# An FFT filter and two MLPs in one kernel: constants on another queue, the first weight pair and the filter's imaginary part loaded later

## The chip, the cores and the metric

One core of a Trainium2 chip runs the whole program in one launch. The metric is the device time of that launch in microseconds (us), as the median of several runs. Engines are named TensorE (PE in profiles), VectorE (DVE), ScalarE (ACT), GpSimd (POOL) and SyncE (SP, which here issues DMAs).

## The reference, cut to what matters

```python
# x: (2, 3008, 256); filt_r, filt_i: (1505, 256); w_in: (256, 2048); w_out: (2048, 256)
X = np.fft.rfft(x, axis=1)
y = np.fft.irfft(X * (filt_r + 1j * filt_i)[None], n=3008, axis=1)
x = y.reshape(6016, 256)
h = x @ w_in                       # first MLP
x = np.maximum(0.01 * h, h) @ w_out
h = x @ w_in2                      # second MLP, its own weights
out = np.maximum(h, 0.0) ** 2 @ w_out2
```

The MLP weights arrive as double precision numbers; the kernel receives them as pairs of 32-bit words.

## The kernel before, in words

The kernel has a filter phase and an MLP phase, and the MLP phase starts as soon as the filter's last results are there.

**Filter phase.** The transform of length 3008 is done as 47 x 64. The work is cut into 32 units: 16 groups of 16 channels (`q`), two batches each, in the order of `units`. A loop over passes `s` (L639) runs the units as a pipeline, so that pass `s` holds different stages of several units:

- `load_x(s + 3)`: SP issues the input of a unit three passes ahead, as two DMAs (L509), into one of four buffers.
- `stage_a(s)` (L538): TensorE's input transform, which needs the input; `stage_r(s)` (L545): VectorE transposes the result (tile `bin`).
- `stage_b(s - 1)` (L550): TensorE, into `px`, with the constant `cb`; `stage_s(s - 1)`: ScalarE copies `px` (L558 in two halves or L560), and VectorE multiplies it with the filter's real part `fr` (L562).
- `stage_2(s - 2)` (L568): GpSimd multiplies the copy with the imaginary part `fi`; `stage_y(s - 2)` (L575) adds the products for some units.
- `stage_i(s - 3)` (L580, L582): TensorE's inverse transform, with the constants `ci` and `cs`; `stage_t(s - 4)` (L589): VectorE transposes the result into `zin`.
- from the middle on also `stage_o` (L596, with the constant `dd`) and `stage_w`: the last transform and its copy, which yields the MLP's input.

The imaginary part needs a sign for each frequency and group before it is used. For groups 0 to 3 that is one product with the constant `sg` in `sign_f` (L530, on VectorE for groups 1 and 2, otherwise on GpSimd); for the larger pieces it is 24 ScalarE steps per piece in `sign_k` (L534). `FI` says which groups form a piece and in which pass it is loaded (L521); `SIGN` says in which pass its sign steps begin and how many a pass has.

**Weights.** Each of the eight weight pairs of an MLP is converted from double precision to single precision and split into a high and a low part. `load_w` (L179, SP) loads one half of a pair, 512 KB, into one buffer per half. `narrow_w` gives the steps: `size` (L200, ScalarE: absolute value), `upper` (L204, L205, VectorE), `signed` (L208, VectorE), `exp` (L213, VectorE), `low` (L219, VectorE; it then has SP load the same half of the next pair), `add` (L225) and `sums` (L230 to L233), then `hi` (L258, ScalarE) and `lo` (L262). The first five pairs are converted during the filter phase.

**What sets the order.** Every engine works through its own instructions in the order in which the program writes them. A clock with four ticks a pass (`tick("F")`) puts the steps of the conversions between the stages: a step goes at the start tick of its pair (`STARTS`) plus its offset in the table `NARROW_F`, and each tick issues the steps that are due:

```python
STARTS = (0, 24, 53, 76, 101)
NARROW_F = dict(
    size0=8, upper0=10, signed0=13, exp0=17, low0=18, size1=18, add0=21, upper1=22, sums=26, signed1=26,
    hi_i=32, exp1=32, low1=33, lo_i=34, add1=40, hi_o=45, lo_o=46,
)
```

Ahead of the loop SP issues the first table `ra` (L490), the inputs of units 0 to 4, the constants (L621, L622, L626, L627, L634), the first pieces of `fr` and `fi`, and both halves of the first weight pair.

**MLP phase.** TensorE multiplies blocks of up to 512 tokens with the weights in three products each (`up`, L342, and `down`, L444), and ScalarE, VectorE and GpSimd prepare and finish the operands around them.

Of the kernel before, what the change touches and what calls it, by code (L numbers as in the profile page):

```python
# [43 lines left out]
SWAP_V = (3, 16, 17, 18, 20, 21, 25, 26, 27, 29, 30)  # L44


FI = ((2, 4, 2), (4, 8, 2), (8, 16, 7))
SGN = (1, 2)
SIGN = ((4, 8, 4, 4), (8, 16, 9, 3))


H0 = 3
# [6 lines left out]


TM = 8
STARTS = (0, 24, 53, 76, 101)
STARTS_1 = (0, 16, 32)
NARROW_F = dict(
    size0=8, upper0=10, signed0=13, exp0=17, low0=18, size1=18, add0=21, upper1=22, sums=26, signed1=26,
# [77 lines left out]
def fft_filter_then_two_mlps(  # L143
# [15 lines left out]
    nc = tc.nc  # L159
# [17 lines left out]
    def load_w(layer, p, k):  # L177
        raw = ws_p.tile([P, 512, 2], I32, tag=f"wraw{k}", name=f"wraw{k}")
        nc.sync.dma_start(  # L179
            raw.rearrange("p c t -> p (c t)"),  # L180
            w_src[layer][p, :, k * 512 : (k + 1) * 512].bitcast(I32),
        )
        w_raw[layer, p, k] = raw
# [90 lines left out]
    def begin(c, steps, table, start):  # L274

        due[c].extend((start + t, steps[name]) for name, t in table.items())
# [21 lines left out]
    def load_macro(l, m, load=True):  # L298
        t0, n = macros[m]
        x = x_p.tile([P, 2, 2, TT], F32, tag="x", name="x")  # L300
        if load:
            nc.sync.dma_start(
                x[:, :, :, :n],
                x_src[l][:, :, t0 : t0 + 2 * n].rearrange("p k (t n) -> p k t n", t=2),
            )
        s = x_p.tile([P, 3, TT], F32, tag="xs", name="xs")
        b11, b12, b21, b22 = (x[:, k, t, :n] for k in range(2) for t in range(2))
        t1, t2, t4 = (s[:, k, :n] for k in range(3))
        x_ops[l, m] = {}
        x_f32[l, m] = {"b11": b11, "b12": b12, "b21": b21, "b22": b22, "t1": t1, "t2": t2, "t3": b12, "t4": t4}  # L310
        return x

    def sum_macro(l, m, part, eng):
        t, a, b = (("t1", "b12", "b11"), ("t2", "b22", "t1"), ("t3", "b22", "b12"), ("t4", "b21", "t2"))[part]
        x = x_f32[l, m]
        eng.tensor_tensor(x[t], x[a], x[b], ALU.subtract)
# [147 lines left out]
    with ExitStack() as fctx:  # L464
# [13 lines left out]
        cb = fc.tile([P, P], F32, name="cb")  # L478
        ci = fc.tile([P, P], F32, name="ci")
        cs = fc.tile([P, P], F32, name="cs")  # L480
        sg = fc.tile([P, NK], F32, name="sg")
        dd = fc.tile([P, P], F32, name="dd")
# [22 lines left out]
        def load_x(s):  # L505
            b, q = units[s]
            t = xin_p.tile([2 * N1, UC * NJ], F32, tag="xin", name="xin")
            for r0, r1 in ((0, XR), (XR, 2 * N1)):
                nc.sync.dma_start(t[r0:r1], x[b, r0:r1, q * UC * NJ : (q + 1) * UC * NJ])  # L509
            xin[s] = t  # L510

        def load_fr(q):
            fr_sb[q] = f_p.tile([P, UC, NK], F32, tag="fr", name="fr")
            nc.sync.dma_start(fr_sb[q], fr[:, q * UC : (q + 1) * UC, :])
# [17 lines left out]
        def sign_k(q0, q1, k):  # L532
            t = fi_of(q0, q1)[:, :, k]
            nc.scalar.activation(t, t, AF.Copy, scale=sg[:, k : k + 1])  # L534

        def stage_a(s):
            pa = ps_a.tile([P, UC, NJ], F32, tag="pa", name="pa")
            nc.tensor.matmul(  # L538
                pa.rearrange("p c n -> p (c n)"), ra[: 2 * N1], xin.pop(s), start=True, stop=True
            )  # L540
            pas[s] = pa
# [6 lines left out]
        def stage_b(s):  # L548
            px = ps_x.tile([P, UC, NK], F32, tag="px", name="px")
            nc.tensor.matmul(px, cb, bin_.pop(s)[:, :, :NK], start=True, stop=True)  # L550
            xps[s] = px
# [49 lines left out]
        def stage_w(h, j, eng):  # L601
            pi = pis.pop((h, j))[:, :, : 2 * N1]
            copy = (lambda d, s: nc.scalar.activation(d, s, AF.Copy)) if eng is nc.scalar else eng.tensor_copy  # L603
            t0, nt = j * TO, TO
            if t0 + nt <= 2 * TT:
                copy(x0[:, h, t0 : t0 + nt].rearrange("p (i t) -> p i t", i=4), pi)
                return
            o = xw_p.tile([P, TO], F32, tag="xo", name="xo")
            copy(o.rearrange("p (i t) -> p i t", i=4), pi)
            a = max(0, 2 * TT - t0)  # L610
            if a:
                nc.gpsimd.tensor_copy(x0[:, h, t0 : t0 + a], o[:, :a])
            nc.sync.dma_start(xt[:, h, t0 + a : t0 + nt], o[:, a:])
# [2 lines left out]
        TO = 8 * N1  # L616
        NO = NT // TO
        x0 = load_macro(0, 0, load=False).rearrange("p k t n -> p k (t n)")
        load_x(0)
        load_x(1)  # L620
        nc.sync.dma_start(cb, c_cb)  # L621
        nc.sync.dma_start(sg, c_sg)  # L622
        load_fr(0)
        load_fi(0, 1)
        load_x(2)
        nc.sync.dma_start(ci, c_ci)  # L626
        nc.sync.dma_start(cs, c_cs)  # L627
        load_x(3)
        load_w(0, 0, 0)
        load_fr(1)  # L630
        load_fi(1, 2)
        load_x(4)
        load_w(0, 0, 1)
        nc.sync.dma_start(dd, c_dd)  # L634
        n = len(units)
        h0 = w0 = 0
        for k, t in enumerate(STARTS):
            begin("F", narrow_w(0, k, f"F{k}"), NARROW_F, t)
        for s in range(n + 4):  # L639
            if 2 <= s < n - 3:  # L640
                load_x(s + 3)
            if s < n:
                stage_a(s)
            if 1 <= s <= n:
                stage_b(s - 1)
            if s > n // 2 + H0 and w0 < h0:
                stage_w(0, w0, nc.scalar)
                w0 += 1
                if w0 == 5:
                    sum_macro(0, 0, 0, nc.gpsimd)  # L650
            tick("F")
            if 4 <= s:
                stage_t(s - 4)
            if 2 <= s <= n + 1:
                stage_2(s - 2)
            tick("F")
            if s < n:
                stage_r(s)
            if 2 <= s <= n + 1:
                stage_y(s - 2)  # L660
            tick("F")
            if 1 <= s <= n:
                stage_s(s - 1)
            if 3 <= s <= n + 2:
                stage_i(s - 3)
            if s % 2 == 0 and s // 2 + 2 < NU:
                load_fr(s // 2 + 2)
            for i, (a, b, t) in enumerate(FI):
                if s == t:
                    load_fi(a, b)  # L670
            if s % 2 == 0 and s // 2 < FI[1][0]:
                sign_f(s // 2)
            for q0, q1, t, c in SIGN:
                for k in range(max(0, (s - t) * c), min(NK, (s - t + 1) * c)):
                    sign_k(q0, q1, k)
            if s >= n // 2 + H0:
                for k in range(1 if s < n else DRAIN[s - n]):
                    if h0 < NO:
                        stage_o(0, h0, ps_a, "pa")
                        h0 += 1  # L680
            tick("F")
# [120 lines left out]
```

## Time and profile before

| | us |
|---|---|
| median of 3 runs | 1157.0 |
| lowest and highest run | 1156.37 and 1157.23 |
| the profiled execution | 1158.98 |
| its span, first to last instruction | 1157.2 |
| TensorE busy | 1135.9 (98%) |
| GpSimd, VectorE, ScalarE busy | 764.9, 654.0, 649.7 |

The rows of a profile come from one execution. A busy time is the sum of an engine's instructions in a stretch. An idle time that stands with an instruction is what its engine waited ahead of it, with the instruction or DMA that ended the wait. The chain of waits goes back from the last instruction, at each step to what released it or to the one ahead of it on its engine. A granted clock of 1.00 is TensorE's full 2.4 GHz, 0.50 is 1.2 GHz.

### The profile page before, as it was taken

The page shows a single profiled execution, that of the slowest core. Times are in us where ns is not written, and L with a number is a line of the kernel's source. Part 1 is how long each engine was busy: PE and PEld are TensorE (multiplying, and loading weights), DVE is VectorE, ACT ScalarE, POOL GpSimd, SP SyncE. Part 2 cuts the span into 40 slices and gives each one's busy share as a digit, 9 for nine tenths or more (in the row PEclk, how much of TensorE's full clock was granted, in tenths as well). Part 3 has the DMA queues.
Part 4 walks back from the last instruction along what each step waited for, and adds up shares of the span by engine and source line. Part 5 has one row for each costly group of instructions (what it writes and reads, how often), then busy time and mean ns, then how long its engine had stood idle before and what let it go on. Part 6 is the DMA issues. An engine that isn't in the chain of part 4 may idle for free.

```text
span 1157.2 us, 14009 instructions
## 1 busy us (share of the span) xinstructions
PE 1135.9 (98%) x4800; PEld 908.9 (79%) x4800; DVE 654.0 (57%) x865; ACT 649.7 (56%) x1209; POOL 764.9 (66%) x617
## 2 busy tenths in 40 slices
PE   8899999999999999999999999999999999999998
PEld 4467987778888878778888788788888788788887
DVE  6999658774674765666644643533534434435432
ACT  3854355564554655654656665655656556556554
POOL 3968458985975965966868855656647556557544
PEclk8999999999999999999999899999999999999999
DMA  8544212111121130130123210100200200200100
GB/s 237 181 132 155 95 59 91 38 66 67 62 95 59 44 132 19 44 132 1 43 69 112 75 71 1 47 25 1 73 1 1 71 1 1 71 1 1 37 1 34
DMA packets 32070, 70.68 MB, mean 61 GB/s; under 512 B 4192, under 2 KB 14528, under 8 KB 31872
## 3 DMA queue, kind: packets, MB, share of 16 engines
q1 hardware_dynamic: 32000, 69.81, 18.4%
q8 instruction: 37, 0.61, 0.2%
q14 instruction: 33, 0.27, 0.1%
HBM read 46.59 MB, written 23.20 MB: 60 GB/s over the span
## 4 chain that ended last, share of the span: by engine, by line
PE 84%; DVE 6%; POOL 2%; issue 2%; ACT 1%; DVEq 0%; POOLq 0%; ACTq 0%
PE py L444 42%; PE ph L342 37%; PE pi L596 4%; PE pa L538 1%; PE px L550 1%; DVE zin L589 1%; POOL gp L365 1%; DVE h L376 1%; PE zps L580 1%; DVE wm L219 1%; DVE wm L204 1%; POOL xop L327 1%; DVE bin L545 0%; DVE v L376 0%; DVE u L376 0%
## 5 line engine op out<-in xcount | busy, mean ns | idle before, releaser
L365 POOL TENSOR_TENSOR gp<-g,gp 128x512 fp32r<-128x512 f32 (+1 forms) x384 | 504.8, 1325 | 332.4 <-ACT gp L364 93.5
L444 PE MATMUL py<-gp,wao 128*128 128x512 f32 (+1 forms) x1440 | 358.8, 390 | 0.0
L342 PE MATMUL ph<-xop,wai 128*128 128x512 f32 (+1 forms) x1260 | 322.2, 393 | 5.0 <-DVE v L376 2.5
L444 PEld LDWEIGHTS py<-gp,wao 128*128 128x128 f32 x1440 | 269.9, 187 | 59.5
L342 PEld LDWEIGHTS ph<-xop,wai 128*128 128x128 f32 x1260 | 234.7, 188 | 62.5 <-DVE v L376 6.6
L444 PE MATMUL py<-gp,wbo 128*128 128x512 f32 (+1 forms) x864 | 216.7, 393 | 0.0
L444 PEld LDWEIGHTS py<-gp,wbo 128*128 128x128 f32 x864 | 163.7, 190 | 36.2 <-POOL gp L365 0.2
L342 PE MATMUL ph<-xop,wbi 128*128 128x512 f32 (+1 forms) x756 | 191.0, 391 | 0.1
L342 PEld LDWEIGHTS ph<-xop,wbi 128*128 128x128 f32 x756 | 140.9, 187 | 33.0 <-DVE v L376 0.9
L376 DVE TENSOR_TENSOR u<-ph,p 128x512 f32<-128x512 f32 (+1 forms) x96 | 65.0, 677 | 148.9 <-PE ph L342 148.8
L355 ACT ACTIVATE g<-h 128x512 f32<-128x512 f32 (+1 forms) x144 | 89.1, 619 | 93.0 <-DVE h L376 89.6
L363 ACT ACTIVATE g<-h 128x512 f32<-128x512 f32 (+1 forms) x144 | 89.0, 618 | 87.2 <-DVE h L372 87.2
L376 DVE TENSOR_TENSOR v<-ph,p 128x512 f32<-128x512 f32 (+1 forms) x96 | 65.0, 677 | 119.5 <-PE ph L342 68.7
L361 ACT ACTIVATE r<-ph 128x512 f32<-128x512 f32 (+1 forms) x48 | 28.2, 587 | 110.9 <-PE ph L342 110.9
L356 ACT ACTIVATE gp<-h 128x512 fp32r<-128x512 f32 (+1 forms) x144 | 87.5, 608 | 0.0
L364 ACT ACTIVATE gp<-h 128x512 fp32r<-128x512 f32 (+1 forms) x144 | 87.4, 607 | 0.0
L372 DVE CUSTOM_DVE_ANT_0 h<-ph,p 128x512 f32<-128x512 f32 (+1 forms) x48 | 32.7, 680 | 92.8 <-PE ph L342 92.8
L355 ACT ACTIVATE g<-ph 128x512 f32<-128x512 f32 (+1 forms) x48 | 28.2, 587 | 97.6 <-PE ph L342 95.5
L376 DVE TENSOR_TENSOR h<-ph,p 128x512 f32<-128x512 f32 (+1 forms) x48 | 32.7, 681 | 80.4 <-PE ph L342 80.4
L596 PEld LDWEIGHTS pi<-dd,zin 128*128 128x128 f32 x256 | 59.0, 310 | 3.9 <-ACT xo L603 1.3
L596 PE MATMUL pi<-dd,zin 128*128 128x128 f32 x256 | 57.4, 375 | 0.7 <-DVE zin L589 0.7
L399 ACT ACTIVATE p<-ph 128x512 f32<-128x512 f32 (+1 forms) x96 | 54.7, 570 | 1.4 <-PE ph L342 1.4
(199 smaller groups left out, 1154.8 us busy)
## 6 DMA issues: line engine op xcount, KB each, us to landing
wraw<-in_w SPq DMA_DIRECT2D x32, 512.0 KB
xin<-in_x SPq DMA_DIRECT2D x32, 160.0 KB
xt<-xo SPq DMA_DIRECT2D x26, 188.0 KB
yt<-o SPq DMA_DIRECT2D x16, 256.0 KB
x<-yt SPq DMA_DIRECT2D x4, 1024.0 KB
out<-o SPq DMA_DIRECT2D x16, 256.0 KB
w<-wi SPq DMA_DIRECT2D x8, 448.0 KB
wi<-w SPq DMA_DIRECT2D x8, 448.0 KB
```

Of the source, the lines that this page charges most:

```text
L342: nc.tensor.matmul(ph[:, :n], w[:, i, k], x[:, j, :n], start=(first and a == 0), stop=(a == 2), skip_group_check=True)
L355: nc.scalar.activation(g[:, :n], h[:, :n], AF.Prelu, alpha=0.01)
L356: nc.scalar.activation(t[:, 0, :n], h[:, :n], AF.Prelu, alpha=0.01)
L361: nc.scalar.activation(r[:, :n], h[:, :n], AF.Relu)
L363: nc.scalar.activation(g[:, :n], h[:, :n], AF.Square)
L364: nc.scalar.activation(t[:, 0, :n], h[:, :n], AF.Square)
L365: nc.gpsimd.tensor_tensor(t[:, 1, :n], g[:, :n], t[:, 0, :n].bitcast(F32), ALU.subtract)
L372: nc.vector._custom_dve(dve_ops.TENSOR_ADD_SAT, out=t[:, :n], in0=ph[:, :n], in1=s[:, :n], s0=F32_MAX, s1=0.0)
L376: nc.vector.tensor_tensor(t[:, :n], ph[:, :n], s[:, :n], ALU.add)
L399: nc.scalar.activation(p1[:, :n], ph[0][:, :n], AF.Copy)
L444: nc.tensor.matmul(acc[c, t][:, :n], w[:, j, 2 * f + c], g[:, k, :n], start=(p == 0 and f == t and a == 0), stop=(p == NP - 1 and f != t a ...
L596: nc.tensor.matmul(pi[:, i], zin[h][b][:, :, 4 * g + i], dd, start=True, stop=True)
```

## The change

The five constants `cb`, `sg`, `ci`, `cs` and `dd` are loaded by DMAs that ScalarE issues, ahead of all inputs in the program. The two halves of the first weight pair are loaded in passes 2 and 3 of the loop, behind that pass's input, instead of ahead of the loop. The piece of the imaginary part for groups 4 to 7 is loaded in pass 4 instead of 2, and its sign steps are done 8 a pass from pass 6 instead of 4 a pass from pass 4; the piece for groups 8 to 15 is loaded in pass 8 instead of 7 and its sign steps begin in pass 10 instead of 9. The conversions of the first four pairs begin 6, 5, 2 and 2 ticks later; that of the fifth stays.

```diff
-FI = ((2, 4, 2), (4, 8, 2), (8, 16, 7))
+FI = ((2, 4, 2), (4, 8, 4), (8, 16, 8))
 SGN = (1, 2)
-SIGN = ((4, 8, 4, 4), (8, 16, 9, 3))
+SIGN = ((4, 8, 6, 8), (8, 16, 10, 3))
...
-STARTS = (0, 24, 53, 76, 101)
+STARTS = (6, 29, 55, 78, 101)
+
+LOAD_W = (2, 3)
...
         x0 = load_macro(0, 0, load=False).rearrange("p k t n -> p k (t n)")
+        for t, c in ((cb, c_cb), (sg, c_sg), (ci, c_ci), (cs, c_cs), (dd, c_dd)):
+            nc.scalar.dma_start(t, c)
         load_x(0)
         load_x(1)
-        nc.sync.dma_start(cb, c_cb)
-        nc.sync.dma_start(sg, c_sg)
         load_fr(0)
         load_fi(0, 1)
         load_x(2)
-        nc.sync.dma_start(ci, c_ci)
-        nc.sync.dma_start(cs, c_cs)
         load_x(3)
-        load_w(0, 0, 0)
         load_fr(1)
         load_fi(1, 2)
         load_x(4)
-        load_w(0, 0, 1)
-        nc.sync.dma_start(dd, c_dd)
...
         for s in range(n + 4):
             if 2 <= s < n - 3:
                 load_x(s + 3)
+            if s in LOAD_W:
+                load_w(0, 0, LOAD_W.index(s))
             if s < n:
                 stage_a(s)
```

## Rows read from the trace of the kernel before

**Rows 1.** Busy us by stretch: PE, PEld, DVE, ACT, POOL; granted clock, DMA share, GB/s.

```profile
6.00:14.00 8.00, 6.29 (x16) 2.59 (x15) 2.85 (x5) 1.39 (x3) 1.99 (x2) 1.00 0.88 238
14.00:30.00 16.00, 13.39 (x29) 6.83 (x30) 14.47 (x26) 7.88 (x21) 9.25 (x11) 0.79 0.99 269
30.00:48.00 18.00, 14.71 (x40) 6.97 (x38) 17.93 (x25) 16.08 (x36) 15.77 (x15) 1.00 0.70 225
...
82.00:114.00 32.00, 31.87 (x116) 23.86 (x117) 31.19 (x48) 15.67 (x31) 22.84 (x22) 1.00 0.48 152
...
124.00:1157.00 1033.00, 1024.03 (x4448) 837.30 (x4448) 541.87 (x699) 581.72 (x1071) 680.26 (x533) 1.00 0.14 48
```

**Rows 2.** The chain of waits at the filter's end: start us, us, what.

```profile
123.65 0.64 DVE zin L589
...
124.42 17.83 PE pi L596 x80
```

**Rows 3.** VectorE's timeline: start us, us, what, count, idle before and its end.

```profile
13.79 0.43 DVE L204 TENSOR_SCALAR wm<-wm 128x512 f32<-128x512 f32 x1 [3.64 <-ACT wm L200]
14.26 1.24 DVE L205 TENSOR_SCALAR wb__206<-wm 128x512 int32<-128x512 int32 x1
15.42 0.55 DVE L562 TENSOR_TENSOR t<-px,fr 128x384 f32<-128x384 f32 x1
15.88 0.54 DVE L530 TENSOR_TENSOR fi<-fi,sg 128x384 f32<-128x384 f32 x1
...
16.95 0.70 DVE L545 STREAM_TRANSPOSE bin<-pa 128x512 f32<-128x512 f32 x1
17.58 0.51 DVE L562 TENSOR_TENSOR t<-px,fr 128x384 f32<-128x384 f32 x1
...
20.48 0.56 DVE L562 TENSOR_TENSOR t<-px,fr 128x384 f32<-128x384 f32 x1 [0.25 <-ACT xc L558]
...
23.66 0.72 DVE L545 STREAM_TRANSPOSE bin<-pa 128x512 f32<-128x512 f32 x1 [0.99 <-PE pa L538]
...
25.19 0.43 DVE L205 TENSOR_SCALAR wb__283<-wm 128x512 int32<-128x512 int32 x1
...
29.86 0.56 DVE L562 TENSOR_TENSOR t<-px,fr 128x384 f32<-128x384 f32 x1 [0.20 <-ACT xc L560]
```

**Rows 4.** ScalarE's timeline, same columns.

```profile
7.79 0.49 ACT L560 ACTIVATE xc<-px 128x384 f32<-128x384 f32 x1 [5.77 <-PE px L550]
13.10 0.66 ACT L200 ACTIVATE wm<-wraw 128x512 f32<-128x512 f32 x1 [4.83 <-DMA wraw<-in_w]
...
17.09 0.67 ACT L200 ACTIVATE wm<-wraw 128x512 f32<-128x512 f32 x1 [2.57 <-DMA wraw<-in_w]
...
23.51 1.47 ACT L534 ACTIVATE fi<-fi,sg 128x64 f32<-128x64 f32 x4 [3.07 <-DMA fi<-in_fi]
...
39.14 0.68 ACT L200 ACTIVATE wm<-wraw 128x512 f32<-128x512 f32 x1 [0.81 <-POOL wo L225]
```

**Rows 5.** SP's timeline: when it issues its DMAs.

```profile
7.53 0.36 SPq L179 DMA_DIRECT2D wraw<-in_w  x1
...
9.81 0.36 SPq L179 DMA_DIRECT2D wraw<-in_w  x1
...
13.14 1.34 SPq L509 DMA_DIRECT2D xin<-in_x  x2
...
15.38 0.82 SPq L521 DMA_DIRECT2D fi<-in_fi  x2
```

**Rows 6.** TensorE's timeline: its longest wait in the first 30 us.

```profile
15.71 1.10 PE L538 MATMUL pa<-xin,ra 94*128 94x512 f32 x2 [2.87 <-DMA xin<-in_x]
```

**Rows 7.** Busy us by stretch, columns of rows 1: TensorE's clock.

```profile
15.00:20.00 5.00, 3.39 (x6) 1.68 (x7) 5.00 (x10) 1.19 (x3) 1.53 (x2) 0.67 1.07 334
20.00:25.00 5.00, 5.00 (x10) 2.50 (x10) 3.73 (x7) 1.93 (x6) 2.53 (x2) 0.65 1.03 268
```

**Rows 8.** GpSimd's timeline: the product that runs beside L205 at 14.26.

```profile
14.22 0.99 POOL L568 TENSOR_TENSOR t<-xc,fi 128x384 f32<-128x384 f32 x1 [4.81 <-ACT xc L560]
```

## The prediction, made before the change was run

> **What bounds the kernel now.** I read first the busy time by stretch [rows 1]. From 30 to 48 us VectorE is busy 17.93 of 18 us; from 82 to 114 us VectorE has 31.19 of 32 and TensorE 31.87 of 32; from 124 us to the end TensorE has 1024.03 of 1033. So the last nine tenths are TensorE's own work, and nothing in the change touches them. What the change can move is the moment at which they start. The chain of waits gives that moment [rows 2]: a VectorE transposition of the inverse transform (zin, L589) ends at 124.29 and releases 17.83 us of unbroken TensorE work. Up to there VectorE is the engine without slack, except in the first 30 us: 2.85 of 8 us busy from 6 to 14, and 14.47 of 16 from 14 to 30. The total of VectorE's work in the filter phase is the same before and after. Therefore **the end moves by what VectorE's idle time in the first 30 us gains or loses**, plus whatever makes its instructions longer or opens new idle time later.
>
> Then I read VectorE's timeline to see which wait ends last in that stretch [rows 3]. The largest is 3.64 us ahead of the first step of the first weight conversion (L204, 13.79), released by ScalarE's absolute value L200. That one had itself waited 4.83 us for the first half of the first weight pair, call it w0 [rows 4], which SP had issued at 7.53 [rows 5]. Both engines work in order, so everything that stands behind these steps waits for a weight that the filter does not need. After 13.79 the idle times are 0.25 (20.48), 0.99 (23.66) and 0.20 us (29.86), 1.4 us in all. The 0.99 us are TensorE's: it had waited 2.87 us for an input until 15.71 [rows 6], and from 15 to 25 us its granted clock averages 0.65 to 0.67 [rows 7], which is partly the lower of its two levels, 1.2 GHz.
>
> **The change, part by part.** A pass has four ticks, and the conversion tables count in ticks.
>
> Constants. Five loads leave SP, at about 0.45 us each: (9.81 - 7.53)/5 = 0.456 us between w0 and the second half, w1 [rows 5]. ScalarE issues them before its first copy. It sat idle for 5.77 us until 7.79 [rows 4], and five times 0.45 is 2.3 us, so this costs nothing; without that idle time it would delay the first copy by 2.3 us. The bytes stay the same. A possible hitch is that issues wait on landings: SP's input load at 13.14 [rows 5] went out 0.04 us after w0 had freed ScalarE at 13.10 [rows 4], and w0 is the eighth DMA before it. If ScalarE's five count in the same ring of eight, the second input waits for the first constants to land, which can push the first two transpositions by up to about 1 us. That is taken out of the idle time that still follows, so 0.
>
> w0 and w1. They go from before the start of the loop to passes 2 and 3, and their first use goes 6 ticks later, to passes 3 and 6. Counting DMAs in SP's order, w0 had 15 ahead of it and now has 18 (the first table, six inputs of two pieces, three pieces of the real part, two of the imaginary part). Its issue is then at 7.53 + 3 x 0.456 = 8.9 us. From issue to use w0 took 13.10 - 7.53 = 5.57 us and w1 took 17.09 - 9.81 = 7.28 us [rows 4, 5]. So w0 is usable between 14.5 and 16.2 us; I take the middle, 15.3. VectorE's L204 follows 0.69 us later as before, at 16.0 instead of 13.79: **+2.2 us** (1.4 to 3.1).
>
> What VectorE does before that point. L204 now stands at the head of pass 4 instead of late in pass 2 (passes and units count from 0), so the products of units 1 and 2 (L562, 0.55 and 0.51 us), the sign product of the second piece (L530, 0.54) and the transposition of unit 3 (L545, 0.70) come ahead of it [rows 3]. They sum to 2.3 us; back to back they start up to 0.09 us before the one ahead has ended (15.88 against 15.42 + 0.55), so about 2.0. Their inputs no longer have the weights ahead of them, so they fall into idle time: **-2.0 us**.
>
> The later idle times. After 16.0 us the inputs of units 4 to 6 should be there (unit 4's had w0 ahead of it and now has not), and VectorE carries a backlog. But TensorE has again little to do while VectorE stands at L204: the input transform of unit 4 is soon done, and the next step waits for VectorE's transposition. So a stretch at the lower clock may come again. Of the 1.4 us I take **-1.0** (0 to -1.4).
>
> Imaginary part. The piece for groups 4 to 7 is loaded in pass 4, not 2, and its 24 sign steps on ScalarE go from 4 a pass over passes 4 to 9 to 8 a pass over passes 6 to 8; the piece for groups 8 to 15 is loaded one pass later and signed from pass 10. In the kernel before, ScalarE waited 3.07 us for the first of these [rows 4], issued with another by 16.2 us [rows 5]; moved, it has two passes of time. I cost this at 0, covered by ScalarE's spare time in passes 4, 5 and 9; what it costs uncovered is the second rival.
>
> Later conversions. The second pair starts 5 ticks later, the third and fourth 2, the fifth not at all. The work only shifts within VectorE's unbroken queue, so 0. The weight reloads that SP issues in the low steps, which wait for VectorE, move along; behind them stand inputs loaded three passes ahead. Two margins shrink: the second pair's second absolute value now comes 1 tick after the GpSimd sum that frees its buffer instead of 2, and the fifth's 1 instead of 3. Its like cost ScalarE 0.81 us at 39.14 [rows 4]. Queued behind it are the copies that GpSimd's products and TensorE's next steps wait for; I take 0, with up to +0.8.
>
> Longer instructions. L205 took 1.24 us at 14.26 and 0.43 us at 25.19 [rows 3]; in the first case a GpSimd product had begun at 14.22 and ran 0.99 us [rows 8]. GpSimd works 1.99 of 8 us from 6 to 14 but 9.25 of 16 from 14 to 30 [rows 1], and the first conversion moves into the latter. I take 0, since the sums of this pair on GpSimd move by the same ticks and one of the first three such steps already pays. The Trainium skill (SBUF — State Buffer, Who interferes with whom) says that such VectorE forms and GpSimd share one port pair, and that the later one stands still until the other has finished. The trace's 0.81 us agree; by that rule alone, were all three of the first half's steps caught, the sum below would be 1.6 us worse.
>
> **Sum:** +2.2 - 2.0 - 1.0 = -0.8 us. The profiled execution took 1158.98 us, a span of 1157.2 and 1.8 around it; that is 2.0 over the median of 1157.0. I apply the difference to the median: 1156.2 us. Differences within 0.2% (2.3 us) are about what a measurement of this kernel cannot tell from no change. The forecast's own range runs from 1.4 - 2.0 - 1.4 = -2.0 to 3.1 - 2.0 + 0 = +1.1, and the 0.8 us of the margins: 1155.0 to 1158.9.
>
> **The rivals.** *The weight lands in time.* If w0 is usable at about 13.1 us in spite of its later issue, because 2.5 us of other transfers no longer crowd it, the first term is 0 and the later idle times vanish too: -2.0 - 1.4 = -3.4 us, 1153.6. For it: the DMA's busy share is 0.99 from 14 to 30 us but 0.88 from 6 to 14 [rows 1], so an SP that reaches its loads earlier can fill it sooner. Against it: w0 still has all inputs that it jumped behind ahead of it. A still earlier landing adds up to 1 us, 1152.6.
>
> *ScalarE is late.* In passes 6 to 8 it has 24 sign steps at 1.47/4 = 0.37 us, 8.8 us, three copies at 0.49, one of them in two halves at as much each, 2.0 us, and one absolute value at 0.66 [rows 4]: 11.4 us. VectorE's passes there take (29.86 - 20.48 - 0.99 - 0.20)/3 = 2.7 us [rows 3], 8.2 for three. So ScalarE falls 3.2 us behind. It decides when that is more than the distance from a copy to the transposition that needs its product, about three passes less GpSimd's and TensorE's steps between. Uncovered, -0.8 + 3.2 = +2.4: 1159.4. For it: ScalarE is busy 16.08 of 18 us from 30 to 48 [rows 1], so it catches up slowly. Against it: the distance is longer than 3.2 us.
>
> *It changes nothing*: the gain ahead of 30 us is eaten between 82 and 114, where TensorE has no room [rows 1]. That gives 1157.0 and counts with the forecast.
>
> **How the numbers follow.** The forecast has 0.48 with the null case (same), the early weight 0.32 (faster), late ScalarE 0.20 (slower). The range takes in both rivals, from 1152.6 to 1159.6, which leaves some 0.15 outside.
>
> **What would show it.** L204 first at about 16.0, with a wait still ending on L200; four transpositions and three L562 products before it; ScalarE's wait for the imaginary part gone; zin's release of the unbroken TensorE work near 123.5. Wrong would be: L204 not waiting at all (first rival), VectorE idle between 30 and 50 us behind L558 or L545 (second), or a gap in TensorE's work after 124 us that is not there before.

## The result: slower, and the profile after

The changed kernel takes 1166.1 us (median of 6 runs, 1165.36 to 1166.45) against 1156.7 of the kernel before in the same runs: a ratio of 1.0079, interval 1.0068 to 1.0090, **9.4 us slower**. The forecast was 0.8 us faster, and its range ended at 1159.6.

In the code after the change, the lines named here stand two further down than before (L204 is now L206, L562 is L564). First the chain of waits at the filter's end, which answers to [rows 2]:

```profile
130.78 2.46 DVE wm L221
133.24 0.64 DVE zin L591
134.01 17.82 PE pi L598 x80
```

The last zin starts at 133.24 instead of 123.65 and TensorE's unbroken work at 134.01 instead of 124.42. All 9.6 us are lost ahead of that point. Next the busy time by stretch after the change, columns of [rows 1]:

```profile
6.00:14.00 8.00, 7.47 (x20) 3.79 (x21) 4.41 (x7) 0.98 (x2) 2.99 (x3) 1.00 0.83 245
14.00:30.00 16.00, 11.44 (x27) 5.85 (x27) 12.60 (x20) 6.22 (x16) 7.60 (x8) 0.79 0.76 231
30.00:48.00 18.00, 12.39 (x30) 6.08 (x29) 15.37 (x21) 12.90 (x32) 10.79 (x12) 0.84 0.58 191
48.00:66.00 18.00, 13.90 (x33) 6.83 (x32) 15.62 (x24) 11.91 (x23) 13.05 (x14) 0.88 0.54 147
82.00:114.00 32.00, 31.01 (x113) 22.94 (x112) 30.41 (x45) 15.81 (x31) 23.73 (x22) 1.00 0.44 132
```

The fourth stretch of the kernel before was not shown yet:

```profile
48.00:66.00 18.00, 15.67 (x42) 7.65 (x42) 17.96 (x28) 14.00 (x27) 14.65 (x13) 1.00 0.37 100
```

VectorE (the third pair of numbers) gains 4.41 - 2.85 = 1.56 us from 6 to 14, the gain that the forecast had counted on, and gives back 1.87 from 14 to 30. Then it loses 2.56 us from 30 to 48 and 2.34 from 48 to 66, where it had been without a gap before. TensorE, GpSimd and ScalarE are less busy there too: no engine has become the bound.

Up to the last zin's end (124.88 before, 134.47 after) VectorE's time can be added up from the trace without a rest: the start of the first transposition, the gaps between instructions from there on, and the instructions.

| us | before | after | difference |
|---|---|---|---|
| first transposition starts | 5.93 | 5.61 | -0.32 |
| idle from there to the last zin | 7.70 | 14.22 | +6.52 |
| instructions of the filter | 65.31 | 67.94 | +2.63 |
| instructions of the conversions | 46.51 | 47.26 | +0.75 |
| end of the last zin | 124.88 | 134.47 | +9.59 |

Two thirds are new idle time and one third longer instructions. Of the idle time 6.7 us lie ahead of 30 us before and 7.0 after; behind 30 us it is 1.0 before and 7.2 after. So nearly all of the new idle time comes behind the stretch on which the forecast was worked out. Both parts can be read in the groups of VectorE's instructions to the filter's end (operation, count, busy time, mean ns of one, idle time ahead of them and its releasers). Before:

```profile
L545 DVE STREAM_TRANSPOSE bin<-pa 128x512 f32<-128x512 f32 x32 | 21.9, 686 | 5.2 <-PE pa L538 5.2
L562 DVE TENSOR_TENSOR t<-px,fr 128x384 f32<-128x384 f32 x32 | 17.4, 543 | 1.6 <-ACT xc L558 1.0 <-ACT xc L560 0.6
L575 DVE TENSOR_TENSOR t<-t,t 128x384 f32<-128x384 f32 x11 | 9.5, 863 | 0.0
L204 DVE TENSOR_SCALAR wm<-wm 128x512 f32<-128x512 f32 x10 | 7.5, 750 | 3.6 <-ACT wm L200 3.6
```

After:

```profile
L591 DVE STREAM_TRANSPOSE zin<-zps 128x512 f32<-128x512 f32 x32 | 22.4, 702 | 1.7 <-PE zps L582 1.7
L547 DVE STREAM_TRANSPOSE bin<-pa 128x512 f32<-128x512 f32 x32 | 21.8, 682 | 4.3 <-PE pa L540 4.3
L564 DVE TENSOR_TENSOR t<-px,fr 128x384 f32<-128x384 f32 x32 | 17.3, 542 | 10.3 <-ACT xc L562 7.8 <-ACT xc L560 2.2 <-issue 0.2
L577 DVE TENSOR_TENSOR t<-t,t 128x384 f32<-128x384 f32 x11 | 11.5, 1049 | 0.3 <-POOL t L570 0.3
L206 DVE TENSOR_SCALAR wm<-wm 128x512 f32<-128x512 f32 x10 | 9.4, 939 | 0.0
```

The wait for the absolute value (3.6 us) is gone, as the change would have it. In its place VectorE waits 10.3 us instead of 1.6 in front of the product L564, all but 0.2 of it released by **ScalarE's copy of the same px**. The eleven sums L577 take 2.0 us longer in all, the ten steps L206 1.9. How long such an instruction takes goes with GpSimd: in both profiles the sums that run beside no GpSimd instruction (three before, two after) take 0.51 to 0.52 us, those beside one up to 2.02 us before and 2.16 after.

How that wait comes about, the timelines show twice. First ScalarE, in pass 3 and from pass 8 to 9:

```profile
16.23 0.66 ACT L202 ACTIVATE wm<-wraw 128x512 f32<-128x512 f32 x1 [5.68 <-DMA wraw<-in_w]
16.79 0.47 ACT L562 ACTIVATE xc<-px 128x384 f32<-128x384 f32 x1
...
34.17 2.84 ACT L536 ACTIVATE fi<-fi,sg 128x64 f32<-128x64 f32 x8
36.91 0.66 ACT L202 ACTIVATE wm<-wraw 128x512 f32<-128x512 f32 x1
37.47 0.93 ACT L260 ACTIVATE wai<-wi 128x896 fp32r<-128x896 f32 x1
38.31 0.47 ACT L562 ACTIVATE xc<-px 128x384 f32<-128x384 f32 x1
```

Then VectorE:

```profile
11.96 0.70 DVE L547 STREAM_TRANSPOSE bin<-pa 128x512 f32<-128x512 f32 x1
17.30 0.56 DVE L564 TENSOR_TENSOR t<-px,fr 128x384 f32<-128x384 f32 x1 [4.64 <-ACT xc L562]
17.77 0.85 DVE L206 TENSOR_SCALAR wm<-wm 128x512 f32<-128x512 f32 x1
...
35.88 0.71 DVE L215 TENSOR_SCALAR wo<-wb__320 128x512 int32<-128x512 int32 x1
38.81 0.56 DVE L564 TENSOR_TENSOR t<-px,fr 128x384 f32<-128x384 f32 x1 [2.23 <-ACT xc L562]
39.28 1.83 DVE L221 SCALAR_TENSOR_TENSOR wm<-wraw,wo 128x512 f32<-128x512 uint32 x1
```

And TensorE:

```profile
10.71 0.81 PE L552 MATMUL px<-bin,cb 128*128 128x384 f32 x2
...
33.99 0.81 PE L552 MATMUL px<-bin,cb 128*128 128x384 f32 x2
...
44.66 1.65 PE L552 MATMUL px<-bin,cb 128*128 128x384 f32 x2 [5.56 <-DVE bin L547]
```

At 16.23 ScalarE is released by w0. The copy of unit 2 stands behind that absolute value and VectorE's product of unit 2 behind the copy, 4.64 us idle, although TensorE had finished its px at 11.5. From 34.17 ScalarE works off eight sign steps, an absolute value and a high part in a row, 4.1 us, and only then comes to the px of unit 8, finished at 34.8; VectorE waits again. The transposition that TensorE needs next (L547, at 43.94) is late by that and by the conversion steps and the zin that VectorE does first from 39.28 on, and TensorE stands for 5.56 us. From 42.2 to 49.0 us TensorE's granted clock is 0.50, its lower level of 1.2 GHz, after it had stood since 39.1; that shows in its next L552: 1.65 us instead of 0.81.

A third place is GpSimd, which waits for ScalarE's high part (L260) with the next unit's product behind it:

```profile
53.82 1.27 POOL L264 TENSOR_TENSOR wao<-wo,wao 128x512 fp32r<-128x512 f32 x1 [4.64 <-ACT wao L260]
55.05 1.00 POOL L570 TENSOR_TENSOR t<-xc,fi 128x384 f32<-128x384 f32 x1
```

TensorE's inverse transforms wait for GpSimd behind that (2.06 us idle at 57.51, 2.04 at 61.97), and zin for the second of them (1.51 us at 63.03).

One point on comparing, ahead of the experiments. The profiled execution of the kernel before took 1158.98 us, 2.3 more than the 1156.7 above, and the trace shows where such a difference can arise. The busy time from 650 to 660 us, before:

```profile
650.00:655.00 5.00, 3.31 (x9) 2.41 (x10) 4.25 (x5) 3.10 (x5) 5.00 (x4) 0.66 0.49 144
655.00:660.00 5.00, 5.00 (x17) 4.12 (x16) 1.14 (x2) 1.67 (x3) 3.86 (x3) 0.66 0.00 0
```

The same work ten microseconds later, after:

```profile
660.00:665.00 5.00, 3.31 (x16) 2.44 (x15) 4.54 (x5) 3.00 (x6) 5.00 (x4) 1.00 0.47 144
665.00:670.00 5.00, 5.00 (x24) 4.11 (x22) 3.40 (x4) 4.06 (x9) 4.60 (x4) 1.00 0.04 16
```

TensorE pauses alike where the second MLP begins, but the granted clock fell to 0.66 on average (6.8 us at 1.2 GHz) in the one and stayed at 1.00 in the other. From the last zin to the end of the span it is 1157.2 - 124.9 = 1032.3 us there and 1164.2 - 134.5 = 1029.7 here. So 2.6 us between the two profiles have nothing to do with the filter; for the filter, its end tells more than the profiled execution's whole time. The table below has the filter's end beside the ratio of all runs.

### The profile page after: what moved, and what is told of

Its sections match the earlier page's. It is cut to its first block, busy times and chain, and to the rows that moved or that the text cites. A ratio compares the mean times of both kernels' runs of the same rounds, so it can differ in the third digit from the quotient of the medians.

```text
span 1164.2 us, 14009 instructions
## 1 busy us (share of the span) xinstructions
PE 1135.6 (98%) x4800; PEld 907.8 (78%) x4800; DVE 657.9 (57%) x865; ACT 650.1 (56%) x1209; POOL 764.4 (66%) x617
## 4 chain that ended last, share of the span: by engine, by line
PE 84%; DVE 8%; POOL 2%; issue 2%; ACT 2%; DMA 1%; SPq 0%; DVEq 0%; POOLq 0%; ACTq 0%
PE py L446 41%; PE ph L344 37%; PE pi L598 3%; PE px L552 1%; DVE wm L206 1%; PE pa L540 1%; DMA wraw<-in_w 1%; PE zps L582 1%; DVE wm L221 1%; DVE bin L547 1%; DVE zin L591 1%; POOL gp L367 1%; DVE t L564 1%; DVE h L378 1%; POOL xop L329 0%
```

## The experiments

All kernels compute the whole reference. "Constants alone" is the kernel before with the five constants on ScalarE's queue. "us" is the ratio less one, times 1157. Against constants alone each "us" is 0.6 more. Filter's end and idle time are those of the table above, from one profiled execution each, and have no interval. How far they can scatter is an estimate: e8's runs spread over 7.8 us, and the part behind the filter differs by 3.1 us at most in the twenty profiles (1029.3 to 1032.4), so the filter's ends of two executions of e8 can lie some 5 us apart. A few us between two filter's ends are a sign and no proof.

| kernel | ratio (interval) | us | filter's end | VectorE idle |
|---|---|---|---|---|
| before | 1 | 0 | 124.88 | 7.70 |
| after | 1.0079 (1.0068 to 1.0090) | +9.1 | 134.47 | 14.22 |
| e3 constants alone | 0.9995 (0.9986 to 1.0004) | -0.6 | 123.60 | 7.44 |
| e1 after, old signs | 1.0040 (1.0027 to 1.0053) | +4.6 | 129.85 | 9.03 |
| e2 after, old weights | 1.0034 (1.0019 to 1.0048) | +3.9 | 128.50 | 11.55 |
| e4 weights alone | 1.0058 (1.0041 to 1.0076) | +6.7 | 130.33 | 11.94 |
| e5 constants, ticks | 1.0060 (1.0043 to 1.0076) | +6.9 | 132.30 | 13.93 |
| e6 constants, late load | 1.0030 (1.0017 to 1.0043) | +3.5 | 127.78 | 9.71 |
| e7 constants, burst | 1.0008 (0.9998 to 1.0018) | +0.9 | 125.28 | 7.50 |
| e8 constants, second piece | 1.0006 (0.9991 to 1.0020) | +0.7 | 124.44 | 8.03 |
| e9 constants, whole passes | 1.0030 (1.0019 to 1.0042) | +3.5 | 125.89 | 8.44 |
| e10 after, low part later | 1.0075 (1.0057 to 1.0093) | +8.7 | 130.97 | 10.14 |
| e11 e5, low part later | 1.0054 (1.0033 to 1.0074) | +6.2 | 128.62 | 11.18 |
| e12 after, whole passes | 1.0056 (1.0038 to 1.0074) | +6.5 | 130.40 | 10.29 |
| e13 after, six signs a pass | 1.0071 (1.0055 to 1.0088) | +8.2 | 132.31 | 12.42 |
| e14 after, second piece old | 1.0081 (1.0066 to 1.0096) | +9.4 | 134.30 | 14.00 |
| e15 after, first piece old | 1.0063 (1.0048 to 1.0078) | +7.3 | 131.43 | 12.07 |
| e16 constants, two ticks | 1.0045 (1.0030 to 1.0060) | +5.2 | 129.95 | 9.88 |
| e17 after, product first | 1.0086 (1.0071 to 1.0102) | +10.0 | 135.10 | 23.15 |
| e18 constants, product first | 1.0070 (1.0053 to 1.0087) | +8.1 | 134.72 | 18.74 |

**Which part costs it?** Four kernels take the change apart: all but the signs, all but the weights, the constants alone, the weights alone.

```diff
-FI = ((2, 4, 2), (4, 8, 4), (8, 16, 8))
+FI = ((2, 4, 2), (4, 8, 2), (8, 16, 7))
-SIGN = ((4, 8, 6, 8), (8, 16, 10, 3))
+SIGN = ((4, 8, 4, 4), (8, 16, 9, 3))
```

> The changed kernel with the old load passes and sign steps of the imaginary part (4 a pass from pass 4). Theory S (the bursts of 8 sign steps a pass keep ScalarE's copies, and with them VectorE's products, waiting): most of the 9.4 us comes back, 1157 to 1159 us, and VectorE's wait of 2.2 us at 38.8 us is gone. Rival W (the later first pair and the later conversions cost it): it stays at 1163 to 1166 us.

```diff
-STARTS = (6, 29, 55, 78, 101)
+STARTS = (0, 24, 53, 76, 101)
...
         load_x(3)
+        load_w(0, 0, 0)
...
         load_x(4)
+        load_w(0, 0, 1)
...
-            if s in LOAD_W:
-                load_w(0, 0, LOAD_W.index(s))
```

> The changed kernel with the old load place of the first weight pair and the old start ticks of all conversions; constants on ScalarE's queue and the new sign steps stay. Theory S: still 1162 to 1166 us. Rival W: 1156 to 1159 us, with VectorE's first conversion step back near 13.5 us.

The third is the kernel before with

```diff
+        for t, c in ((cb, c_cb), (sg, c_sg), (ci, c_ci), (cs, c_cs), (dd, c_dd)):
+            nc.scalar.dma_start(t, c)
         load_x(0)
...
-        nc.sync.dma_start(cb, c_cb)
```

and the same for the other four loads on SP.

> The kernel before with the five constants on ScalarE's queue and nothing else. Both theories: within 1 us of before, 1155.5 to 1157.5 us; if the shared ring of landings delays the second input by a microsecond and this reaches the end, 1158.

The fourth is the kernel before with the loads of e2's diff the other way round and `STARTS` of the change.

> The kernel before with the first pair loaded in passes 2 and 3 and the later start ticks, constants on SP and old sign steps. Theory S: 1156 to 1159 us. Rival W: 1163 to 1166 us, the whole of the change's cost.

Measured: the constants are worth nothing that can be told from no change. With them in place the weights part costs 1.0040 - 0.9995 = 0.0045, 5.2 us; the signs part 1.0034 - 0.9995 = 0.0039, 4.5 us; both together 1.0079 - 0.9995 = 0.0084, 9.7 us. **Both parts are at fault, with about half each**, and the ends of the filter say so too (+6.3, +4.9 and together +10.9 over constants alone). No range given for e1 and e2 was met (1161.2 and 1161.1 us lie between the theories); e4, the weights without the constants, lies in W's range (1163.2). e4's interval overlaps e1's, so whether the constants soften the weights part is not shown.

The two parts do not look alike in the trace. Over constants alone e2 idles 4.1 us more, and VectorE's instructions together are as long (111.2 us against 111.3); e1 idles 1.6 us more, and its instructions are 3.6 us longer (114.9). TensorE's clock does not sort the kernels: up to the filter's end it stood at 1.2 GHz for 6.8 us before and 17.0 after the change, but for 10.2 in constants alone, whose filter ends first, and for 3.4 in e11, whose filter ends 3.7 us later than before.

That the parts add up is not a sign of one mechanism: alone, the signs part stalls in another place. In e2 ScalarE:

```profile
28.96 2.83 ACT L534 ACTIVATE fi<-fi,sg 128x64 f32<-128x64 f32 x8 [4.52 <-DMA fi<-in_fi]
```

and VectorE behind it:

```profile
32.20 0.56 DVE L562 TENSOR_TENSOR t<-px,fr 128x384 f32<-128x384 f32 x1 [3.33 <-ACT xc L560]
```

SP issues the piece at 20.80 us there, behind the reload of the weight buffer at 19.93, and it lands too late for ScalarE, which stands 4.52 us. In the changed kernel SP issues it at 16.96, ahead of that reload (26.69), ScalarE's wait for it is gone (the eight steps at 27.23 begin without one), and VectorE's wait at 38.81 stands behind the burst instead. Either way the copies are late.

**Ticks or load, burst or second piece?** All four are on top of constants alone. Later ticks:

```diff
-STARTS = (0, 24, 53, 76, 101)
+STARTS = (6, 29, 55, 78, 101)
```

> Constants on ScalarE's queue and the later start ticks (6, 29, 55, 78, 101); the first pair is loaded at its old place ahead of the loop, old sign steps. Theory L (the late landing of the first pair is what the weights' part costs): VectorE does not wait for the first conversion, 1153 to 1157 us. Rival T (the later ticks put VectorE's conversions beside GpSimd's work and make them longer): 1159 to 1162 us, VectorE's lines L208, L219 and L575 about 3 us longer in sum.

The weight pair loaded late, with old ticks:

```diff
+LOAD_W = (2, 3)
...
-        load_w(0, 0, 0)
...
-        load_w(0, 0, 1)
...
+            if s in LOAD_W:
+                load_w(0, 0, LOAD_W.index(s))
```

> Constants on ScalarE's queue and the first pair loaded in passes 2 and 3, with all start ticks and sign steps as before. Theory L: at least as slow as constants and weights together, 1161 to 1165 us, since every step of the first pair now waits for its load. Rival T: 1157 to 1159 us.

The burst of eight sign steps, with loads where they were:

```diff
-SIGN = ((4, 8, 4, 4), (8, 16, 9, 3))
+SIGN = ((4, 8, 6, 8), (8, 16, 9, 3))
```

> Constants on ScalarE's queue and 8 sign steps a pass from pass 6 for the piece of groups 4 to 7; its load stays in pass 2, the piece of groups 8 to 15 stays as before. Theory B (the burst itself delays ScalarE's copies, on which VectorE's product waits in the same pass): 1159 to 1162 us. Rival F (the later load of the piece, for which ScalarE waited 4.5 us at 28.96 us in the second experiment): 1155.5 to 1157.5 us.

The second piece one pass later:

```diff
-FI = ((2, 4, 2), (4, 8, 2), (8, 16, 7))
+FI = ((2, 4, 2), (4, 8, 2), (8, 16, 8))
-SIGN = ((4, 8, 4, 4), (8, 16, 9, 3))
+SIGN = ((4, 8, 4, 4), (8, 16, 10, 3))
```

> Constants on ScalarE's queue; the piece of groups 8 to 15 is loaded in pass 8 and signed from pass 10 as in the change, the piece of groups 4 to 7 as before. Both theories: 1156 to 1158 us; more would mean that the second piece costs its own part.

Measured: the ticks alone cost 6.9 us with nothing loaded later, no less than ticks and late load together (e1, 4.6; the intervals overlap, and the filter's end is 2.4 us later). The late load alone costs 3.5. So the terms of the weights part do not add: a conversion that starts later can bear a later load (e6's VectorE waits 5.3 us for the absolute value, e1's does not wait for it). The burst and the second piece, each with the first piece loaded at its old place, give 0.9 and 0.7, neither of which can be told from zero (e8's runs spread from 1153.8 to 1161.6) or from constants alone. What no kernel does is to load the first piece late without the burst.

Of the theories, L is out: e5 (1163.3 us) is far above its range. Rival T named the direction, but e5 is above its range too, and longer instructions are the smaller share: T's three lines are 6.3 us longer than in constants alone (32.4 against 26.1), all of VectorE's instructions together only 1.2 (112.5 against 111.3), while idle time is 6.5 us more. e6 (1160.8) and e7 (1158.05) fall between the ranges given for them. The burst in e7 puts eight sign steps, a high part and an absolute value in a row on ScalarE (28.60 to 32.84), as in the changed kernel from 34.17, and VectorE waits 0.99 us behind it and for no copy. So it is not the burst by itself that makes the copies late.

VectorE's waits in e5 (what waits for what: us in all, times, longest):

```profile
DVE t L562 <- ACT xc L560: 5.1, 5, 2.5
DVE bin L545 <- PE pa L538: 4.7, 2, 3.7
DVE fi L530 <- DMA fi<-in_fi: 2.7, 2, 1.8
DVE t L562 <- ACT xc L558: 2.2, 5, 0.6
```

There is no wait for the weight any more, and 5.1 + 2.2 us of waits for copies. The 2.7 us for fi are new: VectorE, without the first conversion to do, runs up to data that the DMAs have not brought yet. In the kernel before, that work filled a stretch bound by transfers (DMA share 0.99 from 14 to 30 us [rows 1]).

**The place in the pass, or the delay itself?** A theory P said that it matters at which tick of its pass each conversion step falls; its rival Q, that any delay costs as much, since the first conversion no longer fills the idle time at the start. On constants alone, whole passes:

```diff
-STARTS = (0, 24, 53, 76, 101)
+STARTS = (4, 28, 53, 76, 101)
```

> Constants on ScalarE's queue, first pair loaded at its old place, old sign steps; the first two pairs start 4 ticks later, which is one whole pass, the others as before. Theory P (it is the place of a step within its pass that costs, since 6 and 5 ticks put it behind other work of its engine; whole passes keep the old neighbours): 1154 to 1157.5 us, GpSimd's wait of 4.1 us at 52 us gone. Rival Q (any later conversion costs, wherever it stands): 1159 to 1162 us.

On the changed kernel, GpSimd's step of pair 0 that waits at 53.82, three ticks later:

```diff
-            begin("F", narrow_w(0, k, f"F{k}"), NARROW_F, t)
+            begin("F", narrow_w(0, k, f"F{k}"), dict(NARROW_F, lo_o=49) if k == 0 else NARROW_F, t)
```

> The changed kernel with one step of the first pair (the low part of its second half, L264 on GpSimd) 3 ticks later, behind the pass's products instead of ahead of them. Theory H (GpSimd's wait of 4.6 us for ScalarE ahead of 53.8 us holds the products behind it, and through TensorE VectorE's transposition at 63 us): 2 to 3 us of the 9.4 come back, 1163 to 1164.5 us. Rival: that wait lies beside other work, 1165.5 to 1167 us.

The same edit on e5:

> The fifth experiment (later ticks alone, 1163.3 us) with the same step 3 ticks later. Theory H: 1160 to 1161.5 us, VectorE's wait of 1.5 us at 61.9 us gone. Rival: 1162.5 to 1164.5 us.

The whole passes of e9 on the changed kernel (`STARTS` from (6, 29, 55, 78, 101) to (4, 28, 53, 76, 101)):

> The changed kernel with start ticks 4, 28, 53, 76, 101 in place of 6, 29, 55, 78, 101; late loads, constants on ScalarE and new sign steps stay. Theory P: the ticks' part comes back, 1160 to 1163 us, what is left being the late landing and the sign steps. Rival Q: 1164 to 1167 us.

Measured: whole passes cost 3.5 us where 6, 5, 2 and 2 ticks cost 6.9 (the intervals are just apart), and 6.5 instead of 9.1 in the changed kernel (they overlap). The filter's end is 6.4 and 4.1 us earlier with whole passes. e9 (1160.3 us) lies in Q's range and outside P's, e12 (1162.6) in P's and outside Q's. Whole passes are also a shorter delay here, 4, 4, 0 and 0 ticks, so these kernels alone do not part the place from the delay; e16 below is the better test. Over constants alone e9 still ends its filter 2.3 us later, and VectorE waits 2.7 us for fi in it as in e5. Another part of e9's 3.5 us lies behind the filter, where its profiled execution, which equals its median, takes 1158.3 - 125.9 = 1032.4 us, as with the slow stretch above.

The low part three ticks later moved the filter's end by 3.5 us in e10 and 3.7 in e11, and the medians by 1.7 and 0.8 (the "us" of the table by 0.4 and 0.7); the ratios' intervals overlap widely. e10 lies in theory H's range, e11 at the edge of the rival's. That GpSimd waits there is shown by the trace; what that costs is not.

**Which piece of the signs, and how small a delay?** The first three are on the changed kernel, the fourth on constants alone. Six sign steps a pass in place of eight:

```diff
-SIGN = ((4, 8, 6, 8), (8, 16, 10, 3))
+SIGN = ((4, 8, 6, 6), (8, 16, 10, 3))
```

> The changed kernel with 6 sign steps a pass over passes 6 to 9 instead of 8 over 6 to 8. Theory B (it is the burst: each ScalarE copy stands behind the signs of the pass ahead, and VectorE's product waits for the copy): 2 to 4 us come back, 1162 to 1164 us, VectorE's wait of 2.2 us at 38.8 us under 1 us. Rival D (the total of ScalarE's work ahead of pass 10 decides, not its rate): 1165 to 1167 us.

The second piece back (load in pass 7, signs from pass 9):

```diff
-FI = ((2, 4, 2), (4, 8, 4), (8, 16, 8))
+FI = ((2, 4, 2), (4, 8, 4), (8, 16, 7))
-SIGN = ((4, 8, 6, 8), (8, 16, 10, 3))
+SIGN = ((4, 8, 6, 8), (8, 16, 9, 3))
```

> The changed kernel with the piece of groups 8 to 15 loaded in pass 7 and signed from pass 9 as before. Theory B: within 1 us of the changed kernel or slower, 1165 to 1168 us, since its signs then follow the burst without a free pass. Rival E (the second piece's later signs cost): 1162 to 1164.5 us.

The first piece back (load in pass 2, signs 4 a pass from pass 4):

```diff
-FI = ((2, 4, 2), (4, 8, 4), (8, 16, 8))
+FI = ((2, 4, 2), (4, 8, 2), (8, 16, 8))
-SIGN = ((4, 8, 6, 8), (8, 16, 10, 3))
+SIGN = ((4, 8, 4, 4), (8, 16, 10, 3))
```

> The changed kernel with the piece of groups 4 to 7 loaded in pass 2 and signed 4 a pass from pass 4 as before, the second piece as in the change. Theory B: 1160.5 to 1162.5 us, as with both pieces undone. Rival E: 1164 to 1167 us.

Two ticks for the first two pairs:

```diff
-STARTS = (0, 24, 53, 76, 101)
+STARTS = (2, 26, 53, 76, 101)
```

> Constants on ScalarE's queue, loads and signs as before, and only the first two pairs 2 ticks later (2, 26, 53, 76, 101). If the first conversion is what fills VectorE's early idle time, a half pass later lets one product and one sign step go ahead of it and costs little: 1155 to 1158 us. If every later tick costs in proportion (6.2 us for 6 and 5 ticks): 1158 to 1160 us.

Measured: undoing the first piece gives back 1.9 us (the intervals overlap; 3.0 by the filter's end), the second nothing, both 4.5 (e1 against after, intervals apart). Six steps a pass give 0.9, within the uncertainty, and shorten VectorE's wait behind the burst from 2.23 to 1.46 us. e14 (1166.0) lies in theory B's range, e13 (1164.91) and e15 (1163.95) lie in no range given for them. That points to the first piece as the one that hurts, and undoing it seems to help more when the second goes too; how the two act on each other stays open.

Two ticks cost 5.2 us, more than either range given for e16 allows (1161.3 us against 1160 at most), and no less than the four of e9 (the intervals overlap; by the filter's end 4.1 us more). A cost in proportion to the delay would be half of e9's, some 1.7 us, and e16's interval begins at 3.5. So the length of the delay alone does not set the cost, which speaks for P. A proof it is not: one and the same cost for both delays, as Q has it, fits both intervals. Of the 6.35 us by which e16 ends its filter later than constants alone, 3.8 are longer instructions of VectorE (115.1 us in all against 111.3) and 2.4 idle time. One of them:

```profile
32.88 2.26 DVE L213 TENSOR_SCALAR wo<-wb__300 128x512 int32<-128x512 int32 x1
```

It ran beside this one of GpSimd:

```profile
32.77 2.09 POOL L262 TENSOR_TENSOR wai<-wi,wai 128x896 fp32r<-128x896 f32 x1 [0.88 <-PE px L550]
```

In the kernel before, the same step (at 30.33) took 0.70 us. The Trainium skill (SBUF — State Buffer, Who interferes with whom) names this form of VectorE's among those that can take the port pair that it shares with GpSimd, where the later one stands still until the other has finished. These two rows agree: the VectorE step, begun 0.11 us after GpSimd's, ends 0.3 us after it.

**Does the copy have to come first?** The wait of VectorE's product for ScalarE's copy is no wait for data: both only read px. The last theory, H1, was that writing the product ahead of the copy frees VectorE and gives most of the loss back. The edit is the same on the changed kernel (e17) and on constants alone (e18):

```diff
+            t1 = s_p.tile([P, UC, NK], F32, tag="t1", name="t1", bufs=4)
+            nc.vector.tensor_tensor(t1, px, fr_sb[units[s][1]], ALU.mult)
             xc = s_p.tile([P, UC, NK], F32, tag="xc", name="xc")
...
-            t1 = s_p.tile([P, UC, NK], F32, tag="t1", name="t1", bufs=4)
-            nc.vector.tensor_tensor(t1, px, fr_sb[units[s][1]], ALU.mult)
```

> The changed kernel with VectorE's product L564 written ahead of ScalarE's copy of the same tile. Theory H1 (the copy's lateness reaches VectorE through this product, 10 us of waits in the profile, of which up to 4.6 stand at the first conversion and stay in part): 1160 to 1163.5 us, and no wait of a product on ScalarE is left. Rival H2 (it reaches the end through GpSimd's products and TensorE anyway): 1165 to 1167 us.

> Constants on ScalarE's queue, everything else as before, product ahead of the copy. H1: VectorE has 1.6 us of such waits before, so at best 1154.5 to 1156.5 us, a version ahead of both kernels. H2, or ScalarE now late behind VectorE: 1156.5 to 1159 us.

H1 falls as it was put. e17 is as slow as the changed kernel (1167.2 us, just above H2's range), and e18 makes the good kernel 8.1 us slower (1165.7, far above both of its ranges). ScalarE's waits in e18:

```profile
ACT xc L560 <- DVE t L556: 45.5, 20, 3.6
ACT xc L562 <- DVE t L556: 11.1, 5, 5.6
```

And VectorE's in the same kernel:

```profile
DVE bin L545 <- PE pa L538: 7.7, 5, 3.5
DVE t L575 <- POOL t L568: 4.2, 8, 1.2
DVE wm L204 <- ACT wm L200: 3.7, 3, 2.3
DVE zin L589 <- PE zps L580: 3.1, 2, 2.3
```

The second reader of px still waits for the first, now ScalarE for VectorE (57 us in all, of which 50 after that px was complete), and it comes back to VectorE through GpSimd's products and TensorE. These two kernels also show what e1 to e16 rest on: the dependency between the copy and the product follows the order in which the program writes them. They turn the wait round and do not remove it, so what a kernel without it would take is not known from them.

No kernel here beats both; constants alone are level with the kernel before.

## Why the prediction was wrong, step by step

**Constants: right.** 0 was predicted; e3 gives -0.6 us with an interval that holds zero.

**The first weight pair: right in kind, too small in size.** SP issues w0 at 9.86 (8.9 predicted), ScalarE is released at 16.23 (15.3 predicted, bounds 14.5 to 16.2), L206 runs at 17.77 (16.0 predicted): the term of +2.2 us measured +4.0, its upper bound was 3.1. What was overlooked is that ScalarE's copy of the waiting unit comes behind the absolute value, and VectorE's product behind that copy and ahead of L206. The wait therefore does not end on L206, as the prediction said, but on the product, and is longer, 4.64 us instead of 3.64. [Rows 3] showed that releaser (ACT xc ahead of L562), at 0.25 and 0.20 us; the prediction put both among the idle times that would vanish.

**The later idle times, -1.0 us: they went.** From L206 to 30 us VectorE's timeline shows no wait any more (1.4 us before). Taken together, the first 30 us came near the forecast: 0.3 us more idle time there (7.0 against 6.7), where the forecast had the end 0.8 us earlier. Most of the rest was lost behind them.

**The -2.0 us of work that comes first: it came**, with four transpositions and the products ahead of L206: 1.56 us more VectorE work before 14 us. By 30 us it was gone.

**"The work only shifts within VectorE's unbroken queue, so 0": the step that failed.** e5, which moves the start ticks of the first four pairs on top of constants alone, measures 6.9 us (interval 5.0 to 8.8). That includes the first pair's six ticks, which the prediction had counted with the weights' terms; no kernel here moves the second to fourth pair by themselves, so how the 6.9 us divide among the pairs is open. But e5 idles 6.2 us behind 30 us, constants alone 1.5: the unbroken stretch is where it loses most. The queue was unbroken only because ScalarE's copies, GpSimd's products and TensorE's transforms arrived in time, and they did so in the order that was there. Shifted, the conversions' steps on ScalarE and GpSimd stand ahead of copies and products that VectorE needs within the same pass, and the first conversion no longer fills the stretch that is bound by transfers. The margins (up to +0.8) had been sought in buffers; the cost was in the queues.

**Imaginary part, costed 0: the second term that failed, by about 4.5 us** (e2 over constants alone; 4.5 also between e1 and after). The first half of that step held: in the changed kernel ScalarE waits for no fi. The second half, that ScalarE's spare time covers the burst, held by itself (e7) and not in the changed kernel, where VectorE waits 2.23 us behind it. Without the weights part (e2) the trace shows the later load instead, 4.52 us of ScalarE's. So the term's size is measured, and its way to the filter's end only in part.

**Longer instructions, costed 0 (up to +1.6):** +3.4 us, 2.63 of the filter's and 0.75 of the conversions'. The mechanism was named rightly, at L205 alone; it also met the sums L577 (863 to 1049 ns) and L206 (750 to 939 ns), which overlap with GpSimd's instructions for 8.8 us instead of 6.5 and for 8.6 instead of 7.0.

**The rivals.** "The weight lands in time" is excluded by 16.23. "ScalarE is late" had the right engine and sign, at a chance of 0.20, and the sign of its test came true: VectorE idle behind the copy between 30 and 50 us. Its distance was wrong. It set three passes between a copy and the transposition that needs its product; the wait that the trace of the changed kernel shows is that of VectorE's product for the copy in the same pass, without such a distance. e7 has as long a row of ScalarE's steps and no such wait, so a backlog does not decide by itself either. Its price covered the signs alone, 3.2 against about 4.5 us, and not the conversions. "It changes nothing" fell with it.

**After the filter**, no new gap in TensorE's work appeared, as predicted.

**Open:** how far the weights part is the place in the pass (P) and how far the lost filling work (Q), and how it divides among the pairs; why the two sign pieces hurt more together, and what the late load of the first alone costs; the price of GpSimd's wait for the high part; and what the product's wait for the copy costs, since no kernel here removes it.

## What to carry to other kernels

An engine whose timeline shows no gaps is only free to be rearranged if its inputs have slack: before costing a shift at 0, list for each moved step what stands behind it on its own queue, and which engine needs that in the same pass. A releaser in a row of the profile, even at 0.2 us, is a dependency; when the releasing engine gets more to do, that is where the wait appears. Work that no one needs yet, done in a stretch bound by transfers, is hidden there; moved out of it, it is paid for.

## What the runs showed of the hardware beyond that

Behind the pause of TensorE where the second MLP starts, its clock is at 1.2 GHz for a while in some executions and not in others: in the two profiles shown for 6.8 us and not at all, in e4 for 3.4 us. All twenty profiles sort by it. In the seven without such a stretch the time from the last zin to the end is 1029.3 to 1029.8 us, in the nine with 3.4 us it is 1030.1 to 1031.3, in the four with 6.8 us 1032.0 to 1032.4. That is as much as many changes to this kernel bring, so two single executions can differ by it without any difference in the filter.

And two engines that only read the same px wait for each other in program order, in both directions: VectorE up to 4.64 us for ScalarE in the changed kernel, ScalarE 57 us in all for VectorE in e18. No other tile was tried.
